# Attention tiles emitted further ahead of their output tiles, with a regrouped start, in a fused linear-attention and gated-FFN kernel

## Chip, cores, metric

One core of a Trainium2 chip. The metric is device time in microseconds (us), the median of several executions.

The engines: TensorE does matmuls and accumulates in PSUM, of which this kernel uses eight banks (PE in the profile; PEld is its weight load). VectorE (DVE), ScalarE (ACT) and GpSimd (POOL) do the rest. In these kernels SP only issues DMAs. Each engine works through its own list of instructions, and semaphores order the lists against each other. The granted clock is the share of TensorE's full clock that the profile records as granted; "warm" and "cold" below stand for 1.00 and 0.50 of it.

## The reference

```python
x  = A_x                                    # 1 x 2048 x 512, bf16
xn = layernorm(x)
# A: linear attention, 32 heads of 16
q, k, v = split(xn @ wqkv)
phi(t)  = concat(softmax(t @ w_phi), softmax(-(t @ w_phi)))    # per head, 32 features
kv, z   = phi(k)^T v,  sum_s phi(k)
A       = (phi(q) kv) / (phi(q) z + 1e-6) @ wo
# B: gated FFN, width 1376
B       = (gelu(xn @ w_gate) * (xn @ w_up)) @ w_down
out     = x + A + B
```

## The kernel before

Tokens form 16 tiles of 128 and 4 strips of 512. Work comes in four stages.

1. **Start.** Normalise the tiles, transpose them to `xnT`, fold `w_phi` into the key and query weights (`bd` is `w_phi` laid out for that, and "phi" below is `w_phi`). `rstd` is the reciprocal standard deviation of a tile's rows.
2. **k/q/v stage.** 28 projection units; exponentials on ScalarE, row sums of the keys on GpSimd, scaled values on VectorE, kv products on TensorE.
3. **FFN strips.** A strip has 11 FFN steps (8 matmuls of 512 columns each). While one strip's steps run, the four output tiles of the strip before are made: 4 matmuls with `wo`, 11 with `w_down`.
4. **Tail.** The last four output tiles.

Instructions are recorded in program order per engine, with semaphore waits worked out from buffer reads and writes. So *where* a call is written fixes its place in each engine's list. A function such as `att_pe` or `ffn_post` below only appends to those lists.

One attention tile is a set of matmuls (`att_pe`), then four pieces, then a DMA transpose into `oT`:

```python
def att_dve(t):
    def piece0(): ...   # VectorE: reciprocals of the row sums, products      (reads banks 4-6)
    def piece1(): ...   # VectorE: denominator, its reciprocal, coefficients
    def piece2(): mul(0); mul(1)        # VectorE: multiply banks 4 and 5 by the coefficients
    def piece3():
        mul(2)                          # VectorE: bank 6
        op("pool", ... o_sb = otmp[0:512] + otmp[512:1024])        # GpSimd
        dma("sp", ... dma_start_transpose(oT[:, t % NOT], o_sb))   # SP
    return [piece0, piece1, piece2, piece3]
```

The old strips keep one attention tile in flight, run one piece per FFN step, and flush the rest just before the next attention tile, which stands directly ahead of the output tile:

```python
def att(t):
    att_pe(t)
    pend.extend(att_dve(t))

att(0)
for s in range(1, NST):
    for jf in range(NF):
        J = s * NF + jf
        ffn_pe(J); ffn_post(J)
        if pend: pend.pop(0)()
        if jf in (2, 5, 8, 10):
            t = 4 * (s - 1) + (2, 5, 8, 10).index(jf)
            while pend: pend.pop(0)()        # rest of tile t: pieces, GpSimd add, DMA
            att(t + 1)
            if pend: pend.pop(0)()
            out_pe(t, 7)                     # needs oT of tile t
            out_fin(t, 7, False)
for t in range(12, 16):                      # the tail: attention and output alternate
    ...
```

The old start, in the order in which it is recorded:

```python
load_x(0); load wk; load_x(1); load phi (SP queue); load wv; load_x(2..7); ...
pool: bd = mask8 * wphi                      # ahead of every rstd in GpSimd's list
ln_stats(0); ln_rstd(0, 1); ln_norm(0)       # rstd is one GpSimd instruction
...
proj_k(0, 0)                                 # its row sums: four GpSimd instructions, 2.7 us
ln_stats(2); ln_rstd(2, 1); ln_norm(2); ...
proj_k(1, 1)
ln_stats(3); ln_rstd(3, 1); ln_norm(3); ...
```

The softmax here doesn't subtract the row's maximum and nothing guards it: scores larger than these inputs give would overflow.

Of the kernel before, what the change touches and what calls it, by code (L numbers as in the profile page):

```python
# [6 lines left out]
ALU = mybir.AluOpType  # L7
ACTF = mybir.ActivationFunctionType

P = 128  # L10
# [3 lines left out]
DH = 16  # L14
FF = 1376
NT = 16
NST = 4
NF = 11
# [42 lines left out]
class Sched:  # L61
# [57 lines left out]
    def op(self, ename, fn, reads=(), writes=(), extra=()):  # L119
        E = self.engs[ename]  # L120
        waits = self._resolve(E, self._deps_of(reads, writes, extra))
        E.count += 1
        idx = E.count
        clock = dict(E.known)
        clock[E.name] = idx
        h = _Handle(E.name, idx, E.sem, clock)
        E.ops.append((waits, fn, (E.sem, 1)))
        self._update(h, reads, writes)
        return h

    def dma(self, qname, fn, reads=(), writes=(), extra=()):
        E = self.engs[qname]
        slots, nxt = self.pools[qname]
        slot = slots[nxt % len(slots)]
        self.pools[qname][1] = nxt + 1
        deps = self._deps_of(reads, writes, extra)
        if slot.last is not None:
            deps.append(slot.last)
        waits = self._resolve(E, deps)
        slot.count += 1  # L140
        val = 16 * slot.count
        key = ("d", slot.sid)
        clock = dict(E.known)
        clock[key] = val
        h = _Handle(key, val, slot.sem, clock)
        E.ops.append((waits, fn, (slot.sem, 16)))
        slot.last = h
        self._update(h, reads, writes)
        return h
# [17 lines left out]
def bass_parallel_sum__linear_kernel_hedgehog__glu_gated_geglu__prompt_kernel(  # L167
# [11 lines left out]
    x2 = A_x.flatten_outer_dims()  # L179
    out2 = out.flatten_outer_dims()  # L180

    with ExitStack() as es, nc.allow_low_precision("bf16 softmax factors"):
        def sb(shape, dtype, name):
            return es.enter_context(nc.sbuf_tensor(name, list(shape), dtype))

        bf16 = dt.bfloat16
        f32 = dt.float32


        warm = sb([P, 512], bf16, "warm")  # L190
# [2 lines left out]
        ident = sb([P, 128], bf16, "ident")  # L193
        m8t = sb([P, 8], f32, "m8t")
        mask8 = sb([P, 8], f32, "mask8")
        neghalf = sb([P, 2], f32, "neghalf")

        x_all = sb([P, NT, 512], bf16, "x_all")
        stats = sb([P, NT, 6], f32, "stats")
        mv = sb([P, NT, 2], f32, "mv")  # L200
        vpe = sb([P, NT], f32, "vpe")
        rstd = sb([P, NT], f32, "rstd")
        NXN = 4
        xn_sb = sb([P, NXN, 512], bf16, "xn_sb")
        xnT = sb([P, 4, S_TOK], bf16, "xnT")

# [12 lines left out]
        wqT = hT[:, 0, 0:4, :]  # L219
# [31 lines left out]
        def bank(b):  # L251
            return ps[:, b * 512:(b + 1) * 512]
# [44 lines left out]
        B_ob = bufs("ob", 4)  # L297


        def load_x(t):  # L300
            dma("sp", lambda e, t=t: e.dma_start(x_all[:, t, :], x2[t * P:(t + 1) * P, :]), writes=[B_x[t]])

        load_x(0)
        dma("act", lambda e: e.dma_start(
            wk_nat, A_wqkv[:, 512:1024].rearrange("(i p) c -> p i c", p=P)), writes=[B_wknat])
        load_x(1)
        dma("sp", lambda e: e.dma_start(
            wphi[:], A_w_phi.rearrange("(j hl) d f -> (hl d) j f", j=4)), writes=[B_wphi])
        dma("act", lambda e: e.dma_start(
            wv_sb[:], A_wqkv[:, 1024:1536].rearrange("(i p) c -> p i c", p=P)), writes=[B_wv])  # L310
        for t in range(2, 8):
            load_x(t)
        dma("sp", lambda e: e.dma_start_transpose(wqT, A_wqkv[:, 0:512]), writes=[B_wqT])
        for t in range(8, NT):
# [13 lines left out]
        op("pool", lambda e: e.affine_select(  # L328
            mask8[:], m8t[:], pattern=[[16, 8]], compare_op=ALU.is_ge,
            fill=0.0, base=15, channel_multiplier=-1), reads=[B_m8t], writes=[B_mask8])  # L330
        op("pool", lambda e: e.tensor_tensor(
            bd[:].rearrange("p j (a b) -> p j a b", b=DH),
            mask8[:].unsqueeze(1).unsqueeze(3).to_broadcast([P, 4, 8, DH]),
            wphi[:].unsqueeze(2).to_broadcast([P, 4, 8, DH]),
            op=ALU.mult), reads=[B_mask8, B_wphi], writes=[B_bd])


        def ln_stats(t):
            op("dve", lambda e, t=t: e.bn_stats(stats[:, t, :], x_all[:, t, :]),
# [4 lines left out]
        def ln_rstd(t, n):  # L344
            op("dve", lambda e, t=t, n=n: e.tensor_scalar(
                vpe[:, t:t + n], mv[:, t:t + n, 1], 1e-5, None, op0=ALU.add),
               reads=B_mv[t:t + n], writes=B_vpe[t:t + n])
            op("pool", lambda e, t=t, n=n: e.tensor_tensor(  # L348
                rstd[:, t:t + n], vpe[:, t:t + n], neghalf[:, 0:n], op=ALU.pow),
               reads=B_vpe[t:t + n] + [B_nh], writes=B_rstd[t:t + n])  # L350

        def ln_norm(t):
            k = t % NXN
            op("dve", lambda e, t=t, k=k: e.tensor_scalar(  # L354
                xn_sb[:, k, :], x_all[:, t, :], mv[:, t, 0:1], rstd[:, t:t + 1],
                op0=ALU.subtract, op1=ALU.mult),
               reads=[B_x[t], B_mv[t], B_rstd[t]], writes=[B_xn[k]])
# [242 lines left out]
                op("dve", lambda e, i=i, b=b: e.tensor_copy(w2[:, i, :], bank(b)), reads=[BK[b]], writes=[B_w2[i]])  # L600


        for n in range(8):
            op("pe", lambda e: e.matmul(bank(7), warm[:, 0:128], warm[:], start=True, stop=True),
               reads=[B_warm], writes=[BK[7]] if n == 0 else [])
        ln_stats(0)
        ln_rstd(0, 1)
        ln_norm(0)
        for jj in range(2):
            for j in (2 * jj, 2 * jj + 1):  # L610
                for i in range(4):
                    h = op("pe", lambda e, i=i, j=j, jj=jj: e.transpose(
                        bank16(5 + jj)[:, (j % 2) * 512 + i * 128:(j % 2) * 512 + (i + 1) * 128],
                        wk_nat[:, i, j * 128:(j + 1) * 128], ident[:]),
                        reads=[B_wknat, B_ident], writes=[BK[5 + jj]] if (j % 2 == 0 and i == 0) else [])
            BK[5 + jj].last_write = h
        op("act", lambda e: e.activation(
            wkT[:, 0:2, :], bank16(5).rearrange("p (j c) -> p j c", j=2), ACTF.Copy),
           reads=[BK[5]], writes=[B_wkT[0]])
        op("dve", lambda e: e.tensor_copy(wkT[:, 2:4, :], bank16(6).rearrange("p (j c) -> p j c", j=2)),  # L620
           reads=[BK[6]], writes=[B_wkT[1]])
        xt_pe(0, 2)
        ln_stats(1)
        ln_rstd(1, 1)
        ln_norm(1)
        fold(wkT, B_wkT, wk2, B_wk2, 0, 7, "act")
        fold(wkT, B_wkT, wk2, B_wk2, 1, 0, "dve")
        fold(wkT, B_wkT, wk2, B_wk2, 2, 1, "act")
        fold(wkT, B_wkT, wk2, B_wk2, 3, 5, "dve")
        proj_v(0, 4)  # L630
        xt_pe(1, 3)
        proj_k(0, 0)
        ln_stats(2)
        ln_rstd(2, 1)
        ln_norm(2)
        xt_pe(2, 2)
        proj_k(1, 1)
        ln_stats(3)
        ln_rstd(3, 1)
        ln_norm(3)  # L640
        xt_pe(3, 3)
        proj_k(2, 0)
        v_recip(0)
        v_scale(0, 4)
        for i in range(4):
            fold(wqT, [B_wqT], wq2, B_wq2, i, 2 + i % 2, "act")
        proj_k(3, 1)

        def ln_pair(t):
            ln_stats(t)  # L650
            ln_stats(t + 1)
            ln_rstd(t, 2)
            for tt in (t, t + 1):
                ln_norm(tt)
                xt_dma(tt)

        def big_loads(k):
            if k == 0:
# [13 lines left out]
                dma("pool", lambda e: e.dma_start(  # L672
                    wd_sb[0:96, NF - 1, :], B_w_down[(NF - 1) * P:FF, :]), writes=[B_wdb])

        ln_pair(4)


        units = []
        for s in range(3):
# [2 lines left out]
                units.append(("q", s, m))  # L682
        for m in range(4):
            units.append(("q", 3, m))
        nv = 1
        nln = 6
        nbig = 0
        for u, un in enumerate(units):
            b = u % 2
            if u % 3 == 0 and nln < NT:  # L690
                ln_pair(nln)
                nln += 2
            if un[0] == "k":
                proj_k(un[1], b)
            else:
                proj_q(un[1], un[2], b)
            if u % 4 == 3:
                kv_acc(nv - 1)
                proj_v(nv, 4)
                v_recip(nv)  # L700
                v_scale(nv, 4)
                nv += 1
            if u % 3 == 2 and nbig < 5:
                big_loads(nbig)
                nbig += 1
# [2 lines left out]
            reads=[B_mask8], writes=[B_kvrm])  # L708


        for jf in range(NF):
            ffn_pe(jf)
            ffn_post(jf)
            if nv <= NT:
                kv_acc(nv - 1)
                if nv < NT:
                    proj_v(nv, 4)
                    v_recip(nv)
                    v_scale(nv, 4)
                nv += 1  # L720
                if nv == NT + 1:
                    kv_finish()
        assert nv == NT + 1


        pend = []

        def att(t):
            att_pe(t)
            pend.extend(att_dve(t))  # L730

        att(0)
        for s in range(1, NST):
            for jf in range(NF):
                J = s * NF + jf
                ffn_pe(J)
                ffn_post(J)
                if pend:
                    pend.pop(0)()
                if jf in (2, 5, 8, 10):  # L740
                    t = 4 * (s - 1) + (2, 5, 8, 10).index(jf)
                    while pend:
                        pend.pop(0)()
                    att(t + 1)
                    if pend:
                        pend.pop(0)()
                    out_pe(t, 7)
                    out_fin(t, 7, False)
        for t in range(12, 16):
            if t + 1 < NT:  # L750
                while pend:
                    pend.pop(0)()
                att(t + 1)
            b = (7, 0, 1, 2)[t - 12]
            out_pe(t, b)
            while pend:
                pend.pop(0)()
            out_fin(t, b, True)

        with nc.Block() as block:  # L760
            @block.gpsimd
# [49 lines left out]
```

## Time and profile before

| kernel before | value | read from |
|---|---|---|
| time, median (first chip) | 343.0 us | runs |
| span of the profiled execution | 337.3 us | page |
| TensorE busy, mean granted clock | 71%, 0.86 | page, cores |
| TensorE idle ahead of output tiles, waiting for `oT` | 49.0 us | waits |
| TensorE idle ahead of attention matmuls | 11.4 us | waits |
| first FFN matmul | 91.0 us | timeline |

The two waits, as the waits view gives them (us in total, times, longest):

```profile
PE ps_all L565 <- DMA oT<-o_sb: 49.0, 14, 5.0
...
PE ps_all L496 <- DVE otmp L542: 11.4, 12, 1.3
```

The page of the kernel before. Each digit of the rows below is one of 40 equal slices of the span: busy share in tenths, and for PEclk the granted TensorE clock in tenths.

```profile
span 337.3 us, 2987 instructions
...
PE 239.4 (71%) x1112; PEld 106.6 (32%) x1112; DVE 134.5 (40%) x306; ACT 76.1 (23%) x133; POOL 85.6 (25%) x118
...
PE   6525195499999994959558595958686685944956
...
PEclk9967787899999998969795978789697969877798
```

TensorE is dense only in the middle (slices 9 to 15). To the right of that, low busy digits and low clock digits alternate: that is the strip stage.

The windows view of the kernel before: start and length of a stretch, busy time (and count) of PE, PEld, DVE, ACT and POOL, granted clock, DMA share, GB/s.

```profile
0.00:91.15 91.15, 57.20 (x289) 26.33 (x290) 38.40 (x77) 41.61 (x77) 53.48 (x90) 0.87 0.46 110
91.15:117.86 26.71, 26.71 (x177) 14.41 (x176) 20.91 (x27) 6.46 (x10) 0.00 (x0) 1.00 0.00 1
117.86:307.25 189.39, 136.96 (x568) 57.80 (x567) 62.70 (x169) 27.45 (x47) 26.45 (x23) 0.84 0.07 16
307.25:337.30 30.05, 18.57 (x84) 8.02 (x81) 12.45 (x34) 0.59 (x1) 5.70 (x5) 0.83 0.15 40
```

The second stretch shows what this kernel can do: 26.7 us of work without a gap, at clock 1.00. The third has a clock of 0.84 and idle time.

One output tile of the kernel before, on TensorE's timeline (start, length, engine, line, operation, matmuls merged, and in brackets the idle time before them with what ended it):

```profile
147.88 1.89 PE L565 MATMUL ps_all<-wo_sb,oT 128*128 128x512 bf16 x4 [3.37 <-DMA oT<-o_sb]
149.56 4.33 PE L570 MATMUL ps_all<-wd_sb,hT 128*128 128x512 bf16 x11
153.73 1.03 PE L475 MATMUL ps_all<-xnT,wg_sb 128*128 128x512 bf16 x4
...
158.91 0.58 PE L496 MATMUL ps_all<-kvr,EqT 128*128 128x144 bf16 x6
160.26 0.30 PE L496 MATMUL ps_all<-kvr,EqT 128*128 128x144 bf16 x2 [0.77 <-DVE otmp L542]
```

TensorE waits 3.37 us for the transposed attention tile. Then four `wo` matmuls take 1.89 us, while four gate matmuls of the same size, later, take 1.03 us.

VectorE at the same time, in the kernel before:

```profile
139.68 0.69 DVE L488 TENSOR_TENSOR hT<-gs,ps_all 128x512 bf16<-128x512 bf16 x1 [9.61 <-PE ps_all L475]
140.28 0.18 DVE L530 SCALAR_TENSOR_TENSOR den<-t_sb 128x32 f32<-128x32 f32 x1
...
142.01 1.02 DVE L542 TENSOR_TENSOR otmp<-ps_all,cf 128x384 bf16<-128x384 f32 x2
143.13 0.69 DVE L488 TENSOR_TENSOR hT<-gs,ps_all 128x512 bf16<-128x512 bf16 x1
143.73 0.42 DVE L542 TENSOR_TENSOR otmp<-ps_all,cf 128x256 bf16<-128x256 f32 x1
```

VectorE sat idle for 9.61 us with the pieces of the next attention tile ready to run, because its list had an FFN multiply first. Then it did them at the last moment.

The chain that ended last, at its start (start, length, what):

```profile
1.70 6.19 DMA wphi<-in_A_w_phi_dram
...
16.14 1.16 POOL st L391
...
17.36 0.74 POOL st L393
...
18.17 0.41 POOL st L395
...
18.65 0.29 POOL Ssum L397
18.95 0.52 POOL rstd L348
...
53.54 11.31 DMA xnT<-xn_sb
```

The start first waits for phi (landing at 7.9 us), then the reciprocal deviation of the next tile (`rstd`, 0.5 us) stands behind 2.7 us of row sums, and later transposes share the DMA engines with the FFN weights.

### The profile page before, as it was taken

How to read it: one execution, taken by the hardware profiler on the slowest of the kernel's cores; microseconds unless marked ns; L12 is line 12 of the kernel's file. 1: busy time of each engine (PE TensorE's matmuls, PEld its weight loads, DVE VectorE, ACT ScalarE, POOL GpSimd, SP SyncE). 2: the span in 40 equal slices, each digit the busy share in tenths (PEclk: the TensorE clock that was granted, in tenths of full speed). 3: DMA queues.
4: the chain of work that ended last, by engine and by line, in shares of the span. 5: the costliest groups of instructions: out<-in, count | busy, mean ns of one | idle time of the engine just before them, and what ended most of it. 6: DMA issues, size and time to landing. Idle time of an engine off the chain costs nothing.

```text
span 337.3 us, 2987 instructions
## 1 busy us (share of the span) xinstructions
PE 239.4 (71%) x1112; PEld 106.6 (32%) x1112; DVE 134.5 (40%) x306; ACT 76.1 (23%) x133; POOL 85.6 (25%) x118
## 2 busy tenths in 40 slices
PE   6525195499999994959558595958686685944956
PEld 3303032143455551414223232423232232411422
DVE  1514418664377763324140514134050505154261
ACT  2415072368812230202021110202020211200000
POOL 2244477579600001111120211111120201112120
PEclk9967787899999998969795978789697969877798
DMA  7800119953000000000000100000000001001111
GB/s 226 212 0 0 31 33 266 206 136 85 0 2 0 0 2 16 16 18 16 17 24 8 31 10 23 16 16 16 18 16 16 22 10 31 17 17 28 34 43 36
DMA packets 24590, 14.39 MB, mean 43 GB/s; under 512 B 18464, under 2 KB 23584, under 8 KB 24576
## 3 DMA queue, kind: packets, MB, share of 16 engines
q1 hardware_dynamic: 22448, 8.41, 11.5%
q0 software_dynamic: 1072, 4.75, 4.7%
q10 hardware_dynamic: 1056, 1.05, 1.0%
q8 instruction: 8, 0.13, 0.2%
q14 instruction: 6, 0.05, 0.1%
HBM read 7.91 MB, written 2.10 MB: 30 GB/s over the span
## 4 chain that ended last, share of the span: by engine, by line
PE 60%; DMA 16%; POOL 10%; DVE 7%; ACT 3%; issue 2%; SPq 0%; DVEq 0%; POOLq 0%
PE ps_all L475 23%; PE ps_all L570 16%; DMA oT<-o_sb 10%; PE ps_all L565 8%; POOL o_sb L554 5%; PE ps_all L378 4%; DMA xnT<-xn_sb 4%; PE ps_all L415 4%; DVE otmp L542 3%; ACT Ek L383 3%; DVE hT L488 2%; PE ps_all L402 2%; PE ps_all L447 2%; DMA wphi<-in_A_w_phi_dram 2%; POOL st L391 2%
## 5 line engine op out<-in xcount | busy, mean ns | idle before, releaser
L488 DVE TENSOR_TENSOR hT<-gs,ps_all 128x512 bf16<-128x512 bf16 (+1 forms) x44 | 30.2, 687 | 122.1 <-PE ps_all L475 115.9
L565 PE MATMUL ps_all<-wo_sb,oT 128*128 128x512 bf16 x64 | 27.6, 580 | 49.0 <-DMA oT<-o_sb 49.0
L570 PE MATMUL ps_all<-wd_sb,hT 128*128 128x512 bf16 (+1 forms) x176 | 59.2, 505 | 0.0
L475 PE MATMUL ps_all<-xnT,wg_sb 128*128 128x512 bf16 (+1 forms) x176 | 45.2, 379 | 0.0
L475 PE MATMUL ps_all<-xnT,wu_sb 128*128 128x512 bf16 (+1 forms) x176 | 45.2, 379 | 0.0
L554 POOL TENSOR_TENSOR o_sb<-otmp 128x512 bf16<-128x512 bf16 x16 | 18.4, 1148 | 98.8 <-DVE otmp L542 98.8
L585 POOL TENSOR_TENSOR ob<-y_sb,x_all 128x512 bf16<-128x512 f32 x12 | 13.8, 1152 | 105.4 <-ACT y_sb L583 105.4
L485 ACT ACTIVATE gs<-ps_all 128x512 bf16<-128x512 f32 (+1 forms) x44 | 26.2, 597 | 50.7 <-PE ps_all L475 49.5
L583 ACT ACTIVATE y_sb<-ps_all 128x512 f32<-128x512 f32 x12 | 7.2, 597 | 131.5 <-PE ps_all L570 131.5
L570 PEld LDWEIGHTS ps_all<-wd_sb,hT 128*128 128x128 bf16 (+1 forms) x176 | 22.7, 129 | 38.1 <-issue 30.5
L378 PE MATMUL ps_all<-wk,xnT 128*128 128x512 bf16 x64 | 19.9, 442 | 14.7 <-DMA xnT<-xn_sb 13.1
L565 PEld LDWEIGHTS ps_all<-wo_sb,oT 128*128 128x128 bf16 x64 | 6.7, 125 | 59.9 <-DMA oT<-o_sb 48.0
L431 DVE TENSOR_TENSOR vs<-ps_all,vs 128x1024 bf16<-128x1024 f32 x16 | 19.6, 1227 | 15.0 <-PE ps_all L415 14.9
L475 PEld LDWEIGHTS ps_all<-xnT,wu_sb 128*128 128x128 bf16 (+1 forms) x176 | 17.6, 100 | 20.4
L354 DVE TENSOR_SCALAR xn_sb<-x_all,mv,rstd 128x512 bf16<-128x512 bf16 x16 | 9.7, 639 | 35.7 <-POOL rstd L348 35.7
L475 PEld LDWEIGHTS ps_all<-xnT,wg_sb 128*128 128x128 bf16 (+1 forms) x176 | 17.5, 100 | 20.3 <-issue 0.5
L383 ACT ACTIVATE Ek<-ps_all 128x512 bf16<-128x512 f32 x32 | 17.4, 596 | 28.2 <-PE ps_all L378 28.2
L391 POOL TENSOR_TENSOR st<-Ek 128x512 f32<-128x512 bf16 x16 | 18.4, 1151 | 18.8 <-ACT Ek L383 18.8
L542 DVE TENSOR_TENSOR otmp<-ps_all,cf 128x384 bf16<-128x384 f32 (+1 forms) x48 | 22.2, 505 | 0.1
L496 PE MATMUL ps_all<-kvr,EqT 128*128 128x144 bf16 x128 | 13.7, 228 | 11.8 <-DVE otmp L542 11.4
L402 PE MATMUL ps_all<-xnT,wq 128*128 128x512 bf16 x64 | 17.7, 406 | 0.6 <-ACT EqT L409 0.6
L409 ACT ACTIVATE EqT<-ps_all 128x512 bf16<-128x512 f32 x32 | 17.2, 605 | 2.3 <-PE ps_all L402 2.0
(56 smaller groups left out, 187.2 us busy)
## 6 DMA issues: line engine op xcount, KB each, us to landing
x_all<-in_A_x_dram SPq DMA_DIRECT2D x16, 128.0 KB, 2.9
out_dram<-ob SPq DMA_DIRECT2D x16, 128.0 KB, 1.7
wg_sb<-in_B_w_gate_dram POOLq DMA_DIRECT2D x1, 1376.0 KB, 6.8
wu_sb<-in_B_w_up_dram POOLq DMA_DIRECT2D x1, 1376.0 KB, 10.9
wd_sb<-in_B_w_down_dram POOLq DMA_DIRECT2D x1, 1280.0 KB, 7.2
hT<-in_A_wqkv_dram ACTq DMA_DIRECT2D x1, 512.0 KB, 4.8
wv_sb<-in_A_wqkv_dram ACTq DMA_DIRECT2D x1, 512.0 KB, 6.4
wo_sb<-in_A_wo_dram POOLq DMA_DIRECT2D x1, 512.0 KB, 4.5
```

The costliest lines, as they stand in the source:

```text
L378: h = op("pe", lambda e, i=i, t=t, b=b: e.matmul(bank(b), xnT[:, i, t * P:(t + 1) * P], wk2[:, i, :], start=(i == 0), stop=(i == 3)), read ...
L383: h = op("act", lambda e, t=t, b=b, sig=sig: e.activation(Ek[:, t, sig, :], bank(b), ACTF.Exp, scale=(1.0, -1.0)[sig]), reads=[BK[b]], wri ...
L391: op("pool", lambda e: e.tensor_tensor(v1, ev[:, :, 0:8], ev[:, :, 8:16], op=ALU.add), reads=[B_Ek[t]], writes=[B_st[0]])
L402: h = op("pe", lambda e, i=i, p=p, s=s, b=b: e.matmul(bank(b), wq2[:, i, p * 128:(p + 1) * 128], xnT[:, i, s * 512:(s + 1) * 512], start=( ...
L431: h = op("dve", lambda e, v=v, b=b: e.tensor_tensor(v[:, :, :, 0:DH], bank(b).rearrange("p (h d) -> p h d", d=DH).unsqueeze(1).to_broadcas ...
L475: h = op("pe", lambda e, i=i, s=s, jf=jf, w=w, wt=wt, b=b: e.matmul(bank(b)[0:w, :], wt[:, i, jf * 128:jf * 128 + w], xnT[:, i, s * 512:(s ...
L485: op("act", lambda e, w=w, k=k, J=J: e.activation(gs[0:w, k, :], bank(J % 2)[0:w, :], ACTF.Gelu_apprx_tanh), reads=[BK[J % 2]], writes=[B_ ...
L488: h = op("dve", lambda e, w=w, k=k, J=J, s=s, jf=jf: e.tensor_tensor(hT[0:w, s % 2, jf, :], gs[0:w, k, :], bank(2 + J % 2)[0:w, :], op=ALU ...
L542: op("dve", lambda e, q=q, n=n: e.tensor_tensor(otmp[:, k, q * 384:q * 384 + n * 128].rearrange("p (s h d) -> p s h d", s=n, d=DH), bank(4 ...
L554: op("pool", lambda e: e.tensor_tensor(o_sb[:, k, :], otmp[:, k, 0:512], otmp[:, k, 512:1024], op=ALU.add), reads=B_ot[k], writes=[B_o[k]])
L565: h = op("pe", lambda e, j=j, t=t, b=b: e.matmul(bank(b), oT[:, t % NOT, j, :], wo_sb[:, j, :], start=(j == 0), stop=False), reads=[B_oT[t ...
L570: h = op("pe", lambda e, jf=jf, w=w, s=s, tl=tl, b=b: e.matmul(bank(b), hT[0:w, s % 2, jf, tl * 128:(tl + 1) * 128], wd_sb[0:w, jf, :], st ...
```

## The change

Intent: let an attention tile be finished long before its output tile needs it; take the statistics out from behind the row sums; bring phi in first. The arithmetic stays, with three more warm-up matmuls. The core of the diff:

```diff
+        dma("act", ... wphi ...)                      # phi first, on the ACT queue
         load_x(0)
         dma("act", ... wk_nat ...)
         load_x(1)
-        dma("sp", ... wphi ...)
         dma("act", ... wv_sb ...)
+        load_x(2); load_x(3)
+        load_x(4, extra=[B_wknat.last_write])         # further tiles wait for wk
 # start: bd after the first two rstd; tiles 2-3, 4-7, 8-11, 12-15 get one rstd each
-        proj_k(0, 0)
-        ln_stats(2); ln_rstd(2, 1); ln_norm(2); xt_pe(2, 2)
-        proj_k(1, 1)
-        ...
+        for t in range(4, 8):
+            ln_stats(t)
+        ln_rstd(4, 4)                                 # ahead of all row sums
+        proj_k(0, 0)
+        proj_k(1, 1)
+        for t in range(4, 8):
+            ln_norm(t); xt_dma(t)
 # strips
+        ATT_AT = {0: (8, 10), 1: (1, 3, 5, 7, 9), 2: (0, 2, 4, 6, 9), 3: (0, 2, 4, 6)}
+        OUT_AT = {0: (), 1: (2, 5, 8, 10), 2: (2, 5, 8, 10), 3: (2, 5, 8, 10)}
+        for s in range(NST):
+            for jf in range(NF):
+                ffn_pe(J)
+                for _ in range(2):
+                    if pend: pend.pop(0)()            # two pieces, ahead of the FFN multiply
+                ffn_post(J)
+                ...                                   # kv products and values of late tiles
+                if jf in OUT_AT[s]:
+                    out_pe(outs, 7); out_fin(outs, 7, False); outs += 1
+                if jf in ATT_AT[s]:
+                    att_pe(natt); pend.extend(att_dve(natt)); natt += 1
+        while outs < NT:                              # last four, back to back
+            ...
```

Cut: more `xn_sb` buffers (6 for 4), moved transposes and folds, the order of the kv products. Attention is now written two to five tiles ahead of the next output tile, where the old strips wrote it one ahead.

More of the change, by code (lines that the diff above doesn't have):

```diff
@@ L195, in bass_parallel_sum__linear_kernel_hedgehog__glu_gated_geglu__prompt_kernel @@
         mask8 = sb([P, 8], f32, "mask8")
-        neghalf = sb([P, 2], f32, "neghalf")
+        neghalf = sb([P, 4], f32, "neghalf")
         x_all = sb([P, NT, 512], bf16, "x_all")
@@ L202, in bass_parallel_sum__linear_kernel_hedgehog__glu_gated_geglu__prompt_kernel @@
         rstd = sb([P, NT], f32, "rstd")
-        NXN = 4
+        NXN = 6
         xn_sb = sb([P, NXN, 512], bf16, "xn_sb")
@@ L297, in bass_parallel_sum__linear_kernel_hedgehog__glu_gated_geglu__prompt_kernel, with load_x @@
         B_ob = bufs("ob", 4)
-        def load_x(t):
-            dma("sp", lambda e, t=t: e.dma_start(x_all[:, t, :], x2[t * P:(t + 1) * P, :]), writes=[B_x[t]])
+        def load_x(t, extra=()):
+            dma("sp", lambda e, t=t: e.dma_start(x_all[:, t, :], x2[t * P:(t + 1) * P, :]), writes=[B_x[t]], extra=extra)
+        dma("act", lambda e: e.dma_start(
+            wphi[:], A_w_phi.rearrange("(j hl) d f -> (hl d) j f", j=4)), writes=[B_wphi])
         load_x(0)
@@ L306, in bass_parallel_sum__linear_kernel_hedgehog__glu_gated_geglu__prompt_kernel @@
         load_x(1)
-        dma("sp", lambda e: e.dma_start(
-            wphi[:], A_w_phi.rearrange("(j hl) d f -> (hl d) j f", j=4)), writes=[B_wphi])
         dma("act", lambda e: e.dma_start(
             wv_sb[:], A_wqkv[:, 1024:1536].rearrange("(i p) c -> p i c", p=P)), writes=[B_wv])
-        for t in range(2, 8):
+        load_x(2)
+        load_x(3)
+        load_x(4, extra=[B_wknat.last_write])
+        for t in range(5, 8):
             load_x(t)
@@ L330, in bass_parallel_sum__linear_kernel_hedgehog__glu_gated_geglu__prompt_kernel @@
             fill=0.0, base=15, channel_multiplier=-1), reads=[B_m8t], writes=[B_mask8])
-        op("pool", lambda e: e.tensor_tensor(
-            bd[:].rearrange("p j (a b) -> p j a b", b=DH),
-            mask8[:].unsqueeze(1).unsqueeze(3).to_broadcast([P, 4, 8, DH]),
-            wphi[:].unsqueeze(2).to_broadcast([P, 4, 8, DH]),
-            op=ALU.mult), reads=[B_mask8, B_wphi], writes=[B_bd])
         def ln_stats(t):
@@ L600, in fold, with spin @@
                 op("dve", lambda e, i=i, b=b: e.tensor_copy(w2[:, i, :], bank(b)), reads=[BK[b]], writes=[B_w2[i]])
-        for n in range(8):
-            op("pe", lambda e: e.matmul(bank(7), warm[:, 0:128], warm[:], start=True, stop=True),
-               reads=[B_warm], writes=[BK[7]] if n == 0 else [])
+        def spin(n):
+            for m in range(n):
+                op("pe", lambda e: e.matmul(bank(7), warm[:, 0:128], warm[:], start=True, stop=True),
+                   reads=[B_warm], writes=[BK[7]] if m == 0 else [])
+        spin(11)
         ln_stats(0)
         ln_rstd(0, 1)
+        ln_stats(1)
+        ln_rstd(1, 1)
+        op("pool", lambda e: e.tensor_tensor(
+            bd[:].rearrange("p j (a b) -> p j a b", b=DH),
+            mask8[:].unsqueeze(1).unsqueeze(3).to_broadcast([P, 4, 8, DH]),
+            wphi[:].unsqueeze(2).to_broadcast([P, 4, 8, DH]),
+            op=ALU.mult), reads=[B_mask8, B_wphi], writes=[B_bd])
         ln_norm(0)
+        xt_pe(0, 2)
+        ln_norm(1)
         for jj in range(2):
@@ L616, in bass_parallel_sum__linear_kernel_hedgehog__glu_gated_geglu__prompt_kernel @@
             BK[5 + jj].last_write = h
+        xt_pe(1, 3)
         op("act", lambda e: e.activation(
@@ L621, in bass_parallel_sum__linear_kernel_hedgehog__glu_gated_geglu__prompt_kernel @@
            reads=[BK[6]], writes=[B_wkT[1]])
-        xt_pe(0, 2)
-        ln_stats(1)
-        ln_rstd(1, 1)
-        ln_norm(1)
+        ln_stats(2)
+        ln_stats(3)
+        ln_rstd(2, 2)
+        proj_v(0, 4)
         fold(wkT, B_wkT, wk2, B_wk2, 0, 7, "act")
@@ L629, in bass_parallel_sum__linear_kernel_hedgehog__glu_gated_geglu__prompt_kernel @@
         fold(wkT, B_wkT, wk2, B_wk2, 3, 5, "dve")
-        proj_v(0, 4)
-        xt_pe(1, 3)
+        ln_norm(2)
+        ln_norm(3)
+        xt_pe(2, 6)
+        proj_v(1, 2)
+        xt_pe(3, 7)
+        proj_v(2, 3)
+        for t in range(4, 8):
+            ln_stats(t)
+        ln_rstd(4, 4)
         proj_k(0, 0)
-        ln_stats(2)
-        ln_rstd(2, 1)
-        ln_norm(2)
-        xt_pe(2, 2)
         proj_k(1, 1)
-        ln_stats(3)
-        ln_rstd(3, 1)
-        ln_norm(3)
-        xt_pe(3, 3)
+        for t in range(4, 8):
+            ln_norm(t)
+            xt_dma(t)
         proj_k(2, 0)
@@ L645, in bass_parallel_sum__linear_kernel_hedgehog__glu_gated_geglu__prompt_kernel @@
         for i in range(4):
-            fold(wqT, [B_wqT], wq2, B_wq2, i, 2 + i % 2, "act")
+            fold(wqT, [B_wqT], wq2, B_wq2, i, 5 + i % 2, "act")
         proj_k(3, 1)
-        def ln_pair(t):
+        for t in range(8, 12):
             ln_stats(t)
-            ln_stats(t + 1)
-            ln_rstd(t, 2)
-            for tt in (t, t + 1):
-                ln_norm(tt)
-                xt_dma(tt)
+        ln_rstd(8, 4)
+        v_recip(1)
+        v_scale(1, 2)
+        v_recip(2)
+        v_scale(2, 3)
         def big_loads(k):
@@ L673, in big_loads @@
                     wd_sb[0:96, NF - 1, :], B_w_down[(NF - 1) * P:FF, :]), writes=[B_wdb])
-        ln_pair(4)
         units = []
@@ L684, in bass_parallel_sum__linear_kernel_hedgehog__glu_gated_geglu__prompt_kernel @@
             units.append(("q", 3, m))
-        nv = 1
-        nln = 6
+        nv = 3
+        nk = 0
         nbig = 0
@@ L689, in bass_parallel_sum__linear_kernel_hedgehog__glu_gated_geglu__prompt_kernel @@
             b = u % 2
-            if u % 3 == 0 and nln < NT:
-                ln_pair(nln)
-                nln += 2
+            if u in (1, 2, 3, 4):
+                ln_norm(7 + u)
+                xt_dma(7 + u)
+            if u in (5, 6, 7, 8):
+                ln_stats(7 + u)
+                if u == 8:
+                    ln_rstd(12, 4)
+            if u in (10, 11, 12, 13):
+                ln_norm(2 + u)
+                xt_dma(2 + u)
             if un[0] == "k":
@@ L696, in bass_parallel_sum__linear_kernel_hedgehog__glu_gated_geglu__prompt_kernel @@
                 proj_q(un[1], un[2], b)
+            if u < 3:
+                kv_acc(u)
             if u % 4 == 3:
-                kv_acc(nv - 1)
                 proj_v(nv, 4)
@@ L702, in bass_parallel_sum__linear_kernel_hedgehog__glu_gated_geglu__prompt_kernel @@
                 nv += 1
+            if u % 4 == 1 and u > 4:
+                kv_acc(nv - 1)
             if u % 3 == 2 and nbig < 5:
@@ L708, in bass_parallel_sum__linear_kernel_hedgehog__glu_gated_geglu__prompt_kernel @@
             reads=[B_mask8], writes=[B_kvrm])
-        for jf in range(NF):
-            ffn_pe(jf)
-            ffn_post(jf)
-            if nv <= NT:
-                kv_acc(nv - 1)
+        kv_done = nv - 1
+        pend = []
+        natt = 0
+        outs = 0
+        ATT_AT = {0: (8, 10), 1: (1, 3, 5, 7, 9), 2: (0, 2, 4, 6, 9), 3: (0, 2, 4, 6)}
+        OUT_AT = {0: (), 1: (2, 5, 8, 10), 2: (2, 5, 8, 10), 3: (2, 5, 8, 10)}
+        for s in range(NST):
+            for jf in range(NF):
+                J = s * NF + jf
+                ffn_pe(J)
+                for _ in range(2):
+                    if pend:
+                        pend.pop(0)()
+                ffn_post(J)
+                if kv_done < NT:
+                    kv_acc(kv_done)
+                    kv_done += 1
+                    if kv_done == NT:
+                        kv_finish()
                 if nv < NT:
@@ L719, in bass_parallel_sum__linear_kernel_hedgehog__glu_gated_geglu__prompt_kernel @@
                     v_scale(nv, 4)
-                nv += 1
-                if nv == NT + 1:
-                    kv_finish()
-        assert nv == NT + 1
-        pend = []
-        def att(t):
-            att_pe(t)
-            pend.extend(att_dve(t))
-        att(0)
-        for s in range(1, NST):
-            for jf in range(NF):
-                J = s * NF + jf
-                ffn_pe(J)
-                ffn_post(J)
-                if pend:
-                    pend.pop(0)()
-                if jf in (2, 5, 8, 10):
-                    t = 4 * (s - 1) + (2, 5, 8, 10).index(jf)
-                    while pend:
-                        pend.pop(0)()
-                    att(t + 1)
-                    if pend:
-                        pend.pop(0)()
-                    out_pe(t, 7)
-                    out_fin(t, 7, False)
-        for t in range(12, 16):
-            if t + 1 < NT:
-                while pend:
-                    pend.pop(0)()
-                att(t + 1)
-            b = (7, 0, 1, 2)[t - 12]
-            out_pe(t, b)
-            while pend:
-                pend.pop(0)()
-            out_fin(t, b, True)
+                    nv += 1
+                if jf in OUT_AT[s]:
+                    out_pe(outs, 7)
+                    out_fin(outs, 7, False)
+                    outs += 1
+                if jf in ATT_AT[s]:
+                    assert not pend and kv_done == NT
+                    att_pe(natt)
+                    pend.extend(att_dve(natt))
+                    natt += 1
+        while outs < NT:
+            b = (7, 0, 1, 2)[outs - 12]
+            out_pe(outs, b)
+            out_fin(outs, b, True)
+            outs += 1
         with nc.Block() as block:
```

## The prediction

> What bounds it now: TensorE's order, with three losses.
> (a) Output tiles, 117.9 to 307.3 us (windows view). The last pieces of an attention tile run just before the output tile that needs it. The waits view gives 40.6 us of TensorE waiting there for the transposed attention tile (o_sb to oT by DMA, 12 waits of about 3.4 us) and 11.4 us for the multiplies that free the attention banks. After each wait four wo matmuls take 1.87 to 1.89 us (timeline), against 0.86 us warm; the granted clock is 0.84. The stage holds 33 FFN steps (1.73 us), 12 output tiles (15 x 0.216 = 3.24 us) and 13 attention steps (0.50 us): 102 us at full clock. So 52 us are waits and about 35 us cold clock, as the Trainium skill says ("TensorE: Matmul & The Clock Gate", Part 1: half rate by default, released after about 3.4 us of activity); the trace's mean of 580 ns for wo against 379 ns for FFN matmuls agrees.
> (b) Start, 0 to 91.2 us. The chain goes through wphi landing at 7.9 us, POOL bd, then row statistics (L348) that stand behind 2.7 us of POOL row sums (18.9, 26.2, 36.9, 50.2 us), then an 11.3 us transpose of xn beside the weight loads.
> (c) Tail, 307.3 to 337.3 us: output tiles alternating with attention and DMA waits.
>
> What changes. The arithmetic is the same, with three more warm-up matmuls in a wait.
> Attention leads its output tile by 2 to 6 tiles, two pieces per FFN step, so the DMA's 2.4 us and POOL's 1.15 us hide behind other matmuls. DVE needs 3.0 us per tile plus 0.69 per FFN step, some 21 us against 34 us of TensorE per strip: it fits, with a few stalls of 0.3 us where no output tile stands between two attention tiles. 189 becomes about 105 us. The last four output tiles run back to back: 13 us plus 3 us, against 30.
> Start: wphi first, rstd for four tiles in one POOL instruction ahead of the sums. First row sums still start near 16 us (wk load, folds), but tiles 4 to 11 no longer wait for statistics. ACT (1.09 us per unit) and POOL (2.8 us per k tile) pace the 28 units, from about 24 to 57 us. rstd of tiles 12 to 15 still stands behind k7's sums near 43 us, so their transposes meet the gate and up loads (7 and 11 us): I allow 5 to 8 us. FFN starts near 64 us instead of 91.
> From there TensorE's content is 44 x 1.73 + 7 x 0.47 + 6 x 0.86 + 16 x 0.50 + 16 x 3.24, about 144 us; 91 to 118 us in before shows it can run dense at granted clock 1.00.
>
> Sum: 64 + 144 + 4 bubbles + 3 tail = 215 us span. Runs were 2 to 8 us over the profiled span, so 220 us; range 210 to 240. Faster by over 2%: 0.98; within: 0.01; slower: 0.01.
>
> Right would show as: waits for oT under 5 us in all; granted clock from FFN start above 0.97; wo matmuls near 379 ns; last FFN matmul to end near 16 us; FFN starting at 58 to 72 us; the longest TensorE waits before it for xnT or row sums.
>
> What would make it wrong: the start stays paced by POOL or by transposes behind weight loads (FFN starting near 80: 235 us); the clock not granted over 140 us of dense work; an output store holding up the next transpose in the same in-order queue; DVE pieces delaying the gate multiply, so FFN steps exceed 1.73 us.

## The result, and the profile after

217.9 us (217.3 to 219.1) against 343.0 us on the same chip: ratio 0.635, 95% interval 0.631 to 0.640. A ratio is the mean time of one kernel's fast runs over that of the other's in the same rounds, so it is not quite the ratio of the medians quoted. All outputs here and below were correct.

The page of the kernel after:

```profile
span 216.6 us, 3003 instructions
...
PE 199.5 (92%) x1094; PEld 98.3 (45%) x1115; DVE 134.0 (62%) x302; ACT 75.8 (35%) x133; POOL 83.9 (39%) x114
...
PE   7776399949999999999999999999999999998994
...
PEclk9999969997999999999999999999999999999999
```

DVE's busy time is the same (134.0 against 134.5 us). PE's is 40 us less for the same matmuls, because they ran at a higher granted clock (mean 0.98 against 0.86). Records missing from this trace (PE has 1094, PEld 1115) hardly change that: after_again, the same kernel with 1115 PE records, is busy for 199.2 us.

The windows view of the kernel after, cut at the first FFN matmul, the last kv products and the first of the last four output tiles:

```profile
0.00:66.62 66.62, 54.40 (x311) 26.55 (x317) 43.92 (x77) 40.83 (x76) 51.13 (x84) 0.95 0.55 151
66.62:87.27 20.65, 20.49 (x135) 11.03 (x136) 16.14 (x21) 5.73 (x9) 0.79 (x3) 1.00 0.00 1
87.27:200.36 113.09, 111.53 (x593) 54.97 (x603) 71.16 (x201) 29.23 (x49) 30.87 (x28) 1.00 0.15 32
200.36:216.60 16.24, 13.07 (x59) 5.75 (x60) 2.77 (x4) 0.00 (x0) 1.15 (x1) 1.00 0.12 41
```

An output tile of the kernel after, on TensorE's timeline:

```profile
150.68 0.66 PE L493 MATMUL ps_all<-kvr,EqT 128*128 128x144 bf16 x8
...
153.77 1.03 PE L472 MATMUL ps_all<-xnT,wu_sb 128*128 128x512 bf16 x4
154.63 1.03 PE L562 MATMUL ps_all<-wo_sb,oT 128*128 128x512 bf16 x4
155.49 2.54 PE L567 MATMUL ps_all<-wd_sb,hT 128*128 128x512 bf16 x10
157.87 1.03 PE L472 MATMUL ps_all<-xnT,wg_sb 128*128 128x512 bf16 x4
```

No bracket stands anywhere: TensorE did not wait. The `wo` group takes 1.03 us, like its neighbours. (The trace lacks one matmul record of this tile; "x10" is 11.)

The first and the last of TensorE's longer waits in the kernel after (us in total, times, longest):

```profile
PE ps_all L444 <- DVE vs L428: 6.6, 2, 3.5
...
PE ps_all L562 <- ACT y_sb L580: 0.8, 1, 0.8
```

The wait for `oT` is gone from the list. The largest that is left is the kv products waiting for scaled values, in the k/q/v stage. The 0.8 us are a wait for a free PSUM bank.

### The profile page after: what moved, and what is told of

Same layout as the page of the kernel before. It is cut to its first block, busy times and chain, and to the rows that moved or that the text cites. A ratio compares the mean times of both kernels' runs of the same rounds, so it can differ in the third digit from the quotient of the medians.

```text
span 216.6 us, 3003 instructions
## 1 busy us (share of the span) xinstructions
PE 199.5 (92%) x1094; PEld 98.3 (45%) x1115; DVE 134.0 (62%) x302; ACT 75.8 (35%) x133; POOL 83.9 (39%) x114
## 4 chain that ended last, share of the span: by engine, by line
PE 78%; DVE 13%; DMA 3%; POOL 2%; issue 2%; ACT 1%; ACTq 0%; DVEq 0%
PE ps_all L472 32%; PE ps_all L567 18%; PE ps_all L562 6%; PE ps_all L399 5%; PE ps_all L412 5%; PE ps_all L375 4%; PE ps_all L493 4%; PE ps_all L444 4%; DVE stats L336 3%; DMA hT<-in_A_wqkv_dram 3%; DVE xn_sb L351 2%; DVE vs L428 2%; POOL rstd L345 1%; DVE otmp L539 1%; DVE mv L338 1%
## 5 line engine op out<-in xcount | busy, mean ns | idle before, releaser
L472 PE MATMUL ps_all<-xnT,wu_sb 128*128 128x512 bf16 (+1 forms) x170 | 44.5, 379 | 0.3
L567 PE MATMUL ps_all<-wd_sb,hT 128*128 128x512 bf16 (+1 forms) x171 | 40.4, 379 | 0.3
L567 PEld LDWEIGHTS ps_all<-wd_sb,hT 128*128 128x128 bf16 (+1 forms) x176 | 17.2, 98 | 20.8
L472 PEld LDWEIGHTS ps_all<-xnT,wg_sb 128*128 128x128 bf16 (+1 forms) x176 | 17.0, 100 | 16.6
L539 DVE TENSOR_TENSOR otmp<-ps_all,cf 128x384 bf16<-128x384 f32 (+1 forms) x48 | 21.5, 504 | 0.0
L375 PE MATMUL ps_all<-wk,xnT 128*128 128x512 bf16 x61 | 17.0, 405 | 0.6 <-ACT Ek L380 0.3
L412 PE MATMUL ps_all<-wv_sb,xnT 128*128 128x512 bf16 x61 | 16.2, 387 | 0.7 <-DMA wv_sb<-in_A_wqkv_dram 0.6
L444 PE MATMUL ps_all<-vs,Ek 128*128 128x136 bf16 x128 | 10.8, 230 | 6.6 <-DVE vs L428 6.6
L562 PE MATMUL ps_all<-wo_sb,oT 128*128 128x512 bf16 x62 | 16.0, 379 | 0.8 <-ACT y_sb L580 0.8
L351 DVE TENSOR_SCALAR xn_sb<-x_all,mv,rstd 128x512 bf16<-128x512 bf16 x16 | 12.1, 797 | 4.8 <-POOL rstd L345 4.8
```

The source lines that it names most:

```text
L375: h = op("pe", lambda e, i=i, t=t, b=b: e.matmul(bank(b), xnT[:, i, t * P:(t + 1) * P], wk2[:, i, :], start=(i == 0), stop=(i == 3)), read ...
L412: h = op("pe", lambda e, i=i, t=t, b=b: e.matmul(bank(b), xnT[:, i, t * P:(t + 1) * P], wv_sb[:, i, :], start=(i == 0), stop=(i == 3)), re ...
L444: h = op("pe", lambda e, t=t, i=i, sig=sig, p=p, b=b, st=st: e.matmul(bank(b)[:, (i % 3) * GV:(i % 3 + 1) * GV], Ek[:, t, sig, p * 128:(p ...
L472: h = op("pe", lambda e, i=i, s=s, jf=jf, w=w, wt=wt, b=b: e.matmul(bank(b)[0:w, :], wt[:, i, jf * 128:jf * 128 + w], xnT[:, i, s * 512:(s ...
L539: op("dve", lambda e, q=q, n=n: e.tensor_tensor(otmp[:, k, q * 384:q * 384 + n * 128].rearrange("p (s h d) -> p s h d", s=n, d=DH), bank(4 ...
L562: h = op("pe", lambda e, j=j, t=t, b=b: e.matmul(bank(b), oT[:, t % NOT, j, :], wo_sb[:, j, :], start=(j == 0), stop=False), reads=[B_oT[t ...
```

## The experiments

The theory: in the strips TensorE lost time in two ways, by waiting for pieces that were emitted too late and by a cold clock after each wait; the start was braked by statistics and phi. Rivals tested: that the parts need each other; that the slow matmuls are slow for a reason other than the clock; that a lead of several tiles, not early pieces, is what is needed; that GpSimd's sums, not the statistics, pace the start.

Two profiled executions (back_only and front_eager) were over 1.5% above the fastest of their kernel and so count as slow. Their profiles are used here for distances between instructions only; times use fast runs.

### One part alone

```diff
 # front_only: the change's lines up to the k/q/v stage, then the old FFN, attention and output loops
 # back_only:  the old lines up to the k/q/v stage, then the change's loops
```

> The change's start (phi first, grouped statistics, reordered k/q/v stage) with the old FFN, attention and output stage. If the two parts add, only the start is gained: FFN begins near 67 us instead of 91, and the time falls by 22 to 28 us, to about 318 us. Rival: the start's gain is partly eaten later (or the later stage gains from it), so the two single parts don't add up to the 125 us of the whole change.

> The old start with the change's FFN, attention and output stage. If the parts add, this carries most of the change: 343 - 125 + 25 = about 243 us, with waits for the transposed attention tile near 0 and granted clock 1.00 after FFN start. Rival (the parts need each other): over 255 us.

The kernel before took 340.6 us beside these. front_only: 309.8 us (ratio 0.907), 31 us less. back_only: 248.1 us (0.725), 92 us less. Together 123 us; the whole change gained 125.1 us in its own rounds and 124.3 us in a later one. The parts add, and about three quarters of the gain is in the strips and the tail.

The start gained more than the 22 to 28 us expected. Its FFN began at 64.3 us. The old start's first FFN matmul stood at 91.0 us in the profile I predicted from, but at 94.5, 95.1 and 95.7 us in the three other kernels here that keep that start. My reading came from the luckiest of four looks. Why it moves by 4 us between executions was not tested.

### Is it the clock?

The wait stays, but TensorE is kept busy in it with dummy matmuls:

```diff
                     if pend:
                         pend.pop(0)()
+                    for m in range(15):
+                        op("pe", lambda e: e.matmul(bank(7), warm[:, 0:128], warm[:], start=True, stop=True),
+                           reads=[B_warm], writes=[BK[7]] if m == 0 else [])
                     out_pe(t, 7)
```

> Kernel before plus 15 dummy matmuls of 512 columns (3.2 us at full clock) ahead of each of the 12 output tiles in the strips, where TensorE waits about 3.4 us for oT; the wait itself stays. If the slow output matmuls are a cold clock after idling: wo matmuls go from 1.88 to about 0.86 us for four, and 12 x 2.5 to 2.9 us = 30 to 35 us are gained though work is added: 308 to 315 us. Rival (they are slow for another reason, such as just-landed data or weight loads; the clock plays no part): same time or slower, 343 us or more.

319.5 us against 340.6 (0.934): 21 us faster with 180 matmuls *more*. One tile of it on TensorE's timeline (L748 are the dummies):

```profile
146.10 0.30 PE L496 MATMUL ps_all<-kvr,EqT 128*128 128x144 bf16 x2 [0.77 <-DVE otmp L542]
146.23 3.40 PE L748 MATMUL ps_all<-warm 128*128 128x512 bf16 x15
150.58 1.04 PE L565 MATMUL ps_all<-wo_sb,oT 128*128 128x512 bf16 x4 [0.95 <-DMA oT<-o_sb]
151.46 2.54 PE L570 MATMUL ps_all<-wd_sb,hT 128*128 128x512 bf16 x11
```

The `wo` group still ends a wait for the DMA (0.95 us of it is visible), but takes 1.04 us instead of 1.89, and the 11 `w_down` matmuls 2.54 instead of 4.33. (In the other eleven tiles 0.1 to 0.2 us of the wait are visible.) From the first output tile to the thirteenth the granted clock is 1.00 here and 0.82 in the kernel before. So the slowness is the clock, not the data that had just landed. The Trainium skill has the rule in "TensorE: Matmul & The Clock Gate", section "Why this matters for your kernels" (no idle gaps of over about 3 us between bursts of matmuls); this run agrees and puts a size on it.

The size was below my 30 to 35 us. From the first output tile's start to the thirteenth's, the kernel before takes 179.9 us, this one 155.4, the kernel after 99.2 (in its second profile; the first lacks a record there). So of the 80.7 us gained there, 24.5 are clock and the other 56 are waiting. The traces bear both out. Timed from start to start, the `wo` and `w_down` matmuls of these twelve tiles took 64.4 us in the kernel before and 39.0 here; and the waits view of the kernel before accounts for 52.0 us of the 56, for `oT` and for banks ahead of these tiles (40.6 and 11.4). Not every tile had been cold to its end: after the waits the clock stood at 0.50 for 3.4 us in some tiles and for 6.8 us in others, and the 11 `w_down` matmuls took from 3.0 to 4.5 us from start to start, against 2.4 warm.

### Is a long lead needed?

One edit to the kernel before. The lead stays one tile:

```diff
         def att(t):
             att_pe(t)
-            pend.extend(att_dve(t))
+            for piece in att_dve(t):
+                piece()
```

> Kernel before with one edit: the four pieces of an attention tile are emitted at once, straight after its matmuls, so that they run on VectorE during the previous output tile; the lead stays at one tile. Theory A (what costs is WHEN the pieces run; a lead of one tile is enough in the strips): waits for oT in the three strips fall from 40.6 us to under 5, the cold clock goes too, strips take about 110 us instead of 189, the tail keeps its waits; time about 343 - 80 = 263 us. Theory B (a lead of two or more tiles is what is needed): most of the 40.6 us of waits stay, time over 310 us.

258.9 us against 340.6 (0.757). This edit alone gains 82 us. `att(t + 1)` stands just ahead of output tile `t`, so the pieces now run while TensorE does that output tile, in the time in which VectorE had been idle for 9.6 us. The twelve output periods sum to 100.3 us, against 99.2 with the long lead. All waits for `oT` come to 8.2 us, in three places: 1.5 us ahead of the first output tile, and 3.3 and 3.5 us in the tail.

```profile
PE ps_all L565 <- DMA oT<-o_sb: 8.2, 3, 3.5
```

So theory A holds: what cost was *when* the pieces ran, not how many tiles they led by.

The long lead pays in the tail. From the thirteenth output tile's start to TensorE's end, eager_pieces takes 21.1 us, the changed kernel 13.1. back_only, which has the long lead on the same old start, took 248.1 us on this chip: 10.8 us less than eager_pieces, of which the tail is 8.0. The same was tried with the new start:

> The change's start with the old one-tile lead, the pieces emitted at once. If a lead of one suffices in the strips and the longer lead pays only in the tail: 12 strip periods sum to about 100 us as in the changed kernel (99), the last four output tiles take about 25 us from the first to the last start and end instead of 13, and the time is 216 + 11 = about 227 us. Rival (the longer lead matters in the strips when the start is fast): over 232 us.

225.7 us (0.661; 217.5 for the changed kernel beside it). Output periods 101.4 us and tail 22.1 us, in a slow profile (99.2 and 13.1 in the changed kernel): the tail again carries most of the 8.2 us that the short lead costs. The tail is 3 us shorter than I had expected, and the strips 1 us longer.

### What braked the start?

```diff
 # late_rstd: statistics of tiles 4-7 back behind the first four key tiles
-        for t in range(4, 8):
-            ln_stats(t)
-        ln_rstd(4, 4)
         proj_k(0, 0)
         ...
         proj_k(3, 1)
+        for t in range(4, 8):
+            ln_stats(t)
+        ln_rstd(4, 4)
+        for t in range(4, 8):
+            ln_norm(t); xt_dma(t)
```

> The changed kernel with the statistics of tiles 4 to 7 emitted after the first four key tiles, so that their rstd stands behind POOL's row sums as it did before. Theory (statistics standing behind the sums were the brake of the old start): rstd of tiles 4 to 7 comes near 29 us instead of 17, the first projection of tile 4 near 34 us instead of 27.5, time 5 to 9 us longer (223 to 227). Rival (POOL's sums or ScalarE's exponentials pace this stage, the statistics have slack): within 2 us of the changed kernel.

223.6 us; the changed kernel beside it 216.1. The 7.4 us lie in the range expected of the theory. TensorE stood idle for 10.7 us in one piece:

```profile
PE ps_all L375 <- DMA xnT<-xn_sb: 10.7, 1, 10.7
```

`rstd` of tiles 4 to 7 ran at 27.1 us, behind four tiles' row sums, instead of 15.2 us. The release shown is the transpose; the cause is three steps back.

```diff
-        dma("act", ... wphi ...)
         load_x(0)
         dma("act", ... wk_nat ...)
         load_x(1)
+        dma("sp", ... wphi ...)
         ...
         op("pool", ... mask8 ...)
+        op("pool", ... bd = mask8 * wphi ...)      # ahead of the first rstd
         ln_stats(0); ln_rstd(0, 1)
         ln_stats(1); ln_rstd(1, 1)
-        op("pool", ... bd = mask8 * wphi ...)
```

> The changed kernel with phi loaded third on the SP queue and its POOL product emitted ahead of the first rstd, as before. If phi's landing was on the start's chain: first rstd near 9.6 us instead of 4.9, first row sums near 19.5 instead of 17.1 us, time 2 to 4 us longer (220 to 222). Rival (wk's landing at 7.1 us covers it): under 1 us.

222.5 us, 6.4 us more: twice what I expected. Phi landed at 7.8 us, so the first `rstd` ran at 8.9 us instead of 4.3. I had counted only that delay against wk's landing. But the new order on TensorE puts the transpose of tile 0 ahead of wk's transposes, so with phi late everything behind it waits too, and cools: the 16 transposes of wk then took 1.91 us instead of 1.06. The first row sums began at 21.3 us instead of 16.2. "Phi first" and "tile 0 first" are one decision. The edit moves two things, the load of phi and its product on GpSimd; which of them costs more was not separated.

The two edits make up 14 of the 31 us that the start gained. The rest (the grouped statistics of the other tiles, the order of the k/q/v stage, the `xn_sb` buffers) was not tested apart. In the traces TensorE waited 12.6 us for normalised tiles and 13.1 us for their DMA transposes in the kernel before, 1.3 and 0 in the kernel after.

### A version that beats both

The kernel after still loses time between 20 and 50 us. A first attempt:

```diff
-        NVS = 3
+        NVS = 6                                # value buffers
-            b = u % 2
+            b = u % 4                          # projection banks
-            if u in (10, 11, 12, 13):  ln_norm(2 + u); xt_dma(2 + u)
+            if u in (12, 13, 14, 15):  ln_norm(u); xt_dma(u)
-            if u < 3:                  kv_acc(u)
+            if u in (3, 5, 7):         kv_acc((u - 3) // 2)
-            if u % 4 == 1 and u > 4:   kv_acc(nv - 1)
+            if u % 4 == 1 and u > 8:   kv_acc(nv - 2)
```

> The changed kernel with the k/q/v stage loosened: four PSUM banks in turn for the projections instead of two, six value buffers instead of three with the kv products emitted one or more tiles later, and the normalisation of tiles 12 to 15 two units later, so that the value scaling no longer stands behind rstd on VectorE. The 3.5 us and 3.0 us waits of the kv products and the cold clock after them should go and ScalarE's 1.09 us per unit should pace the stage: FFN begins near 59 us instead of 66, time 209 to 212 us. Rival (POOL's sums, 2.8 us per tile, pace it through the value scaling): no gain.

The three fast runs took 214.2 to 216.7 us (a fourth was slow), against 215.7 to 217.4 for the changed kernel: the same. TensorE's waits of this kernel from 20 to 52 us show why:

```profile
PE ps_all L375 <- DVE vs L428: 3.6, 1, 3.6
...
PE ps_all L375 <- DMA xnT<-xn_sb: 2.7, 1, 2.7
```

The two old waits were gone and two new ones of the same size stood there. The first was my mistake: the third projection was given a bank that still held values waiting to be scaled. The second: normalising later moved the transposes of tiles 12 to 15 beside the weight loads. Mended:

```diff
-            b = u % 4
+            b = u % 2 if u < 4 else u % 4
 # statistics of tiles 12-15 in units 5 and 6, one rstd there; their normalisation in units 8 to 11
-            b = (7, 0, 1, 2)[outs - 12]
+            b = (0, 1, 2, 7)[outs - 12]        # the first tail tile gets a free bank
```

> The first loosening gained nothing because two new waits took the place of the two old ones: the third projection was put in a bank that still held values not yet scaled (3.6 us), and the later normalisation put the transposes of tiles 12 to 15 wholly beside the weight loads (2.7 us). Here the projections take four banks in turn only from the fifth unit on, and the statistics of tiles 12 to 15 come one key tile earlier so that their normalisation needs no wait; the first of the last four output tiles takes a free bank (0.8 us). If those waits were the loss: FFN begins 3 to 5 us earlier than in the changed kernel, the time is 4 to 6 us shorter (210 to 213 us). Rival (POOL's row sums pace the stage whatever the banks): FFN begins at the same time, and only the 0.8 us of the bank are gained.

212.4 us (212.2 to 213.2) against 217.5 for the changed kernel on the same chip, ratios 0.623 and 0.637 to the kernel before: 5.1 us, or 2.3%, faster, as expected. That is clear of the noise (1.7% to 2.9% by the scatter of the runs), but whether it is over 2% is not. FFN began at 61.2 us instead of 67.2 (63.9 and 66.5 in the changed kernel's other two looks), and the 0.8 us bank wait was gone. So GpSimd's sums were not what paced the stage in the changed kernel. Which of the edits (banks, value buffers, later kv products, earlier statistics) gained how much was not separated. What is left there is 3.8 us of value projections waiting for one bank's scaling and 1.4 us for a transpose. improved2 has the smallest time here.

The changed kernel itself was run twice more, beside these:

> The changed kernel itself, run again beside the other three so that they share a chip. 217 to 219 us, FFN beginning at 64 to 68 us.

It took 216.1 us, with FFN beginning at 63.9 us: both slightly below what was expected.

> The changed kernel once more, so that the next two stand beside it on one chip: 215 to 219 us.

It took 217.5 us.

## Why the prediction was right

- **The sum.** 220 us predicted, 217.9 measured. Predicted span: 64 (start) + 144 + 4 + 3 = 215; measured 216.6, of which 66.5 lie ahead of the first FFN matmul and 150.1 after it (151 predicted). In two other looks FFN began at 63.9 and 67.2 us.
- **Output tiles.** The work was counted from warm durations in the trace, and it ran at them: clock 1.00 after FFN start, no wait for `oT`, `wo` matmuls at 379 ns as predicted. Where two attention tiles fall in one period it took 9.74 to 9.81 us, against 8.92 + 0.50 without a stall: the few 0.3 us stalls that were foretold.
- **The split of the strips' loss** was off in the clock: 52 us of waits and 35 us of cold clock predicted; 56 and 24.5 measured, over a stretch that starts and ends at output tiles. I took the clock as what was left over after counting work and waits. That remainder also held two FFN steps (3.5 us): the window from 117.9 us contains 35 FFN steps, not 33. The other 7 us were not traced. The sum held because it was made from the work that remains, not from the losses, and both losses went.
- **Tail.** "last FFN matmul to end near 16 us" was wrong: 20.3 us. Five output tiles, not four, follow the last FFN matmul, and one waited 0.8 us for a bank. The last four take 16.2 us, as costed. The fifth was counted among the work, so the total did not suffer.
- **Start.** The time was right and one cause was not. I allowed 5 to 8 us because the transposes of tiles 12 to 15 would meet the weight loads. They did not hold TensorE up (0.3 us, for one weight load). What did was VectorE's list, twice: first the value scaling stood behind the statistics of tiles 8 to 11 (3.5 us), then behind the normalisation of tiles 12 and 13, which waited for `rstd` (3.0 us). After both waits the granted clock fell to 0.50 for 3.4 us.

```profile
25.68 1.23 DVE L428 TENSOR_TENSOR vs<-ps_all,vs 128x1024 bf16<-128x1024 f32 x1
...
26.96 0.76 PE L444 MATMUL ps_all<-vs,Ek 128*128 128x136 bf16 x8 [3.54 <-DVE vs L428]
...
42.04 1.03 POOL L345 TENSOR_TENSOR rstd<-vpe,neghalf 128x4 f32<-128x4 f32 x1
...
43.10 2.04 DVE L351 TENSOR_SCALAR xn_sb<-x_all,mv,rstd 128x512 bf16<-128x512 bf16 x2 [2.63 <-POOL rstd L345]
...
45.65 1.23 DVE L428 TENSOR_TENSOR vs<-ps_all,vs 128x1024 bf16<-128x1024 f32 x1
...
46.94 0.65 PE L444 MATMUL ps_all<-vs,Ek 128*128 128x136 bf16 x8 [3.03 <-DVE vs L428]
```

That the allowance came out at the right size for the wrong reason is luck. The prediction's own sign, that the longest waits ahead of the FFN would be for `xnT` or row sums, failed with it. improved2, which changed this order and the banks, began its FFN at 61.2 us, so part of the allowance could be removed.

- **None of the dangers named** came: the clock held at 1.00 for 150 us, FFN steps took 1.73 us on TensorE, stores did not hold up transposes.

## What to carry to other kernels

Where an engine waits for a short chain on other engines, look at what those engines did in the meantime: if they were idle with the work ready, the order of emission is the fault, and one line may mend most of it (82 of 125 us here). An idle gap ahead of matmuls can cost more than its length: here each wait of 3.4 us cost another 2 us of clock. A dummy fill tells the two apart. When a wait is removed, check the waits view again before trusting the gain; the first improved version traded two waits for two others.

## What the Trainium skill lacked or had wrong

- "TensorE: Matmul & The Clock Gate" has the cause and the rule right, and its section "HAM oscillation — how this bites in real kernels" works out what such waits cost in another kernel. It has no test that takes the cold clock away and leaves the wait. Here twelve waits of 3.4 us (with 0.8 to 1.4 us for bank releases just before) cost 24.5 us of clock, 2.0 us a tile, with 11 `w_down` matmuls taking 3.0 to 4.5 us. It also doesn't name the remedy tested here, dummy matmuls in a wait that can't be removed: 21 us gained.
- "SBUF — State Buffer", section "SBUF: two separate sides", says that VectorE, in some of its modes, and GpSimd share a port pair as an exclusive lock held for a whole instruction. The traces fit, though they do not show the mode: a normalisation takes 0.40 us when started with GpSimd idle, but 1.13 us when started 0.07 us after GpSimd's 1.05 us phi product, and the median of the 16 rose from 414 to 874 ns when the change moved most of them beside the row sums (no experiment isolates the lock). The page gives no such figure for this pair of operations.
- "DMA: Bandwidth & Descriptors", section "Rules for kernel authors", says that a transpose beside ordinary DMAs needs nothing. That is about results, and they were right. In time, a transpose of xn landed in 2.4 us alone and in 5.5 to 11.3 us beside the first FFN weight loads (kernel before); no page I read gives that cost.
